# An mLSTM cell followed by mixture-of-depths: TensorE's order written by hand, chunks made ready two steps ahead, gates in one copy

## The chip, the cores and the metric

The kernel runs on one core of a Trainium2 chip. A core has five engines that run side by side, each through its own queue of instructions, and wait for one another by semaphores: TensorE (PE in the profile; its weight loads are listed apart as PEld), VectorE (DVE), ScalarE (ACT), GpSimd (POOL) and SyncE (SP), which here only issues DMAs. The metric is the device time of one execution in microseconds (us); the span of a profile is the part of it from the first to the last instruction of the program.

## What is computed

First an mLSTM cell for 4 batches, 8 heads, 768 positions and a head dimension of 40, then a mixture-of-depths block over rows of 320 (= 8 x 40). Cut to what matters:

```python
for t in range(S):                          # S = 768
    m_new  = maximum(f[t] + m, i[t])
    f_stab = exp(f[t] + m - m_new);  i_stab = exp(i[t] - m_new);  m = m_new
    C = f_stab * C + i_stab * outer(v[t], k[t])        # 40 x 40 per head
    n = f_stab * n + i_stab * k[t]
    y[t] = sigmoid(o[t]) * (C @ q[t]) / maximum(abs(n @ q[t]), 1)
x = y as (4, 768, 320)
scores = x @ w_gate
for b in range(4):
    top = the 128 rows of x[b] with the highest scores
    out[b] = x[b];  out[b, top] += sigmoid(scores[b, top]) * (relu(x[b, top] @ w1) @ w2)   # 320 -> 1024 -> 320
```

## The kernel before

The sequence is cut into chunks of L = 128 positions, so that a batch has NT = 6 chunks and the kernel 24 steps n = (b, c). Within a chunk the recurrence is done as a masked 128 x 128 product per head; between chunks a state C of 41 columns (the 41st carries the normaliser n) is passed on. All the large products are in float32.

**The gates.** `gates(c0, c1)` works for all 32 (batch, head) pairs at once, one pair per partition, by scans on VectorE. Log weights of a pair of positions are the difference of two vectors, a and M. Each is split into three bfloat16 numbers, and the kernel holds the gates four times over (partitions 0 to 127), one copy for each part, so that `operands(u, c)` places them with two matmuls (`pO`, L164), from which ScalarE copies `a_o` (L167) and VectorE makes `M_o` (L168). Three small transpositions (`pc`, L195) turn the remaining factors into columns (`cols`, L197). Gates are set up in three calls: chunk 0, chunks 1 and 2, chunks 3 to 5.

**A step.** `prepare` makes a chunk ready one step ahead: two bfloat16 matmuls `pW` (L220), the exponential `W` on ScalarE (L221), the causal mask on GpSimd (L222), the weighted values `wv` on GpSimd (L227), the transpositions of k and q `pt` (L233) and their copies `T` on ScalarE (L234), and the output gate `so` (L236, L237). `mlstm_chunk` then does:

- `pS` (L250), the product of keys and queries, 64 rows deep; VectorE multiplies it with W into `P` (L252, two instructions);
- `pI` (L261), the part from the state; VectorE scales it into `num` (L264);
- `pC` (L272), the chunk's own part of the next state; GpSimd scales the old state (L275), VectorE adds (L284, in a batch's first chunk a copy, L282);
- `pH` (L289), the part from within the chunk; VectorE adds it to `num` (L293), makes `den` and `rec` (L297 to L300), GpSimd makes `sor` (L302), VectorE makes the row block `x` (L303) and its scores `sc` (L306); GpSimd's queue writes x to the output (L308).

`pI`, `pC` and `pH` share one pool of two PSUM buffers in this order, so that pH takes the buffer of pI once VectorE has read it into `num`. `pt` and `pW` share another pool of two, and all smaller products a third (`ps_m`).

**The second block.** `compare` transposes a chunk's scores (`pb`, L315), ScalarE copies them (L316) and VectorE compares them with the earlier ones (`ge`, L318). Once a batch is complete, during the next batch: `ranks` in step c = 1 (`pcol`, L327; `sel`, L337), `gather` in c = 2 (`pidx`, L347; an indirect DMA brings the 128 rows `xe`, L353), `enter` and the first half of layer 1 in c = 3 (`pX`, L373; `xeT`, L375; `ph`, L386; relu into `hT`, L388), the other half in c = 4, layer 2 in c = 5 (`py`, L394; `ye`, L396; an indirect DMA out, L397). The layer 2 of the third batch is left to the end, where the fourth batch's selection and both its layers follow as a chain.

**What sets the order.** The kernel is written in the Tile framework, which traces the program and then orders the instructions of every engine by priorities and modelled costs. In the kernel before this holds for all engines. TensorE's stream of the kernel before, for instance, mixes transpositions of a later chunk between the `pS` of an earlier one.

Of the kernel before, what the change touches and what calls it, by code (L numbers as in the profile page):

```python
# [27 lines left out]
def kernel(  # L28
# [34 lines left out]
    SLOTS = [(j, min(128, capacity - j)) for j in range(0, capacity, 128)]  # L63
# [3 lines left out]
    AHEAD = 3  # L67

    assert S == NT * L and NT == 6 and D < DP and H == 8 and B == 4 and F_ == NFC * 128 and 0 < capacity < S <= 2048

    const = ctx.enter_context(tc.tile_pool(name="const", bufs=1))
    gate = ctx.enter_context(tc.tile_pool(name="gate", bufs=1))
    ob = ctx.enter_context(tc.tile_pool(name="ob", bufs=2))
# [3 lines left out]
    outp = ctx.enter_context(tc.tile_pool(name="outp", bufs=2))  # L77
    dram = ctx.enter_context(tc.tile_pool(name="dram", bufs=1, space=bass.MemoryType.DRAM))
# [6 lines left out]
    G = [slice(BH * g, BH * (g + 1)) for g in range(4)]  # L85
    f_sb = gate.tile([128, NT, L], FP, name="f_sb")
    i_sb = gate.tile([128, NT, L], FP, name="i_sb")

    def load_f_i(c0, c1):
        for dst, src, eng in ((f_sb, f_gate, nc.sync), (i_sb, i_gate, nc.scalar)):  # L90
            for g in G:
                eng.dma_start(out=dst[g, c0:c1], in_=src.rearrange("b h (c p) -> (b h) c p", p=L)[:, c0:c1])

    ident = const.tile([128, 128], FP, name="ident")
    make_identity(nc, ident)
    load_f_i(0, 1)
# [6 lines left out]
    def load_chunk(b, c):  # L103
        n = (b * NT + c) % NB
        if b * NT + c < NB:
            nc.gpsimd.memset(qk_t[n][:, :, :, D:DP], 0.0)
            nc.gpsimd.memset(v_t[n][:, :, D:DP], 1.0)
        t = slice(c * L, (c + 1) * L)
        for j, src in enumerate((k, q)):
            nc.sync.dma_start(out=qk_t[n][:, j, :, 0:D], in_=src[b, :, t, :].rearrange("h p d -> p h d"))  # L110
        nc.sync.dma_start(out=v_t[n][:, :, 0:D], in_=v[b, :, t, :].rearrange("h p d -> p h d"))
        so = ob.tile([128, H, D], FP, name="so", bufs=NB)
        nc.sync.dma_start(out=so, in_=o_gate[b, :, t, :].rearrange("h p d -> p h d"))
        return qk_t[n], v_t[n], so

    place = [[const.tile([128, 4, 8, 4], BF, name=f"place{x}{u}") for u in range(B // 2)] for x in "Ma"]  # L120
    for j, (own, other, sign) in enumerate(((0, 3, -1.0), (3, 0, 1.0))):
        for u, pl in enumerate(place[j]):
            nc.vector.memset(pl, 0.0)
            nc.vector.memset(pl[0:1, :, other:other + 3, :], 1.0)
            nc.vector.tensor_scalar(out=pl[:, :, own:own + 3, :].rearrange("p g k h -> p k g h"), op0=OP.mult,
                                    in0=ident[:, BH:].rearrange("p (k n g h) -> p k n g h", k=3, g=4, h=4)[:, :, u],
                                    scalar1=sign, scalar2=None)
    which = const.tile([128, 4], FP, name="which")
    nc.vector.tensor_reduce(out=which, in_=ident.rearrange("p (k h) -> p h k", h=4), op=OP.add, axis=AX.X)


    again = const.tile([128, NT, L], BF, name="again")
    low = const.tile([128, NT, L], BF, name="low")
# [4 lines left out]
    F = gate.tile([128, NT, L], FP, name="F")  # L138
    a = gate.tile([128, NT, L], FP, name="a")
    Mg = gate.tile([128, NT, L], FP, name="Mg")  # L140
    m = gate.tile([128, NT + 1], FP, name="m")
    a3 = const.tile([128, NT, L], BF, name="a3")
    M3 = const.tile([128, NT, L], BF, name="M3")

    rest, r, wk = f_sb, F[0:BH], i_sb[0:BH]
    nc.vector.memset(m[:, 0:1], -BIG)
    cols, M_o, a_o = [], {}, {}
# [4 lines left out]
    def split(x3, x, g):  # L152
        nc.vector.tensor_copy(out=x3[:, g], in_=x[:, g])
        nc.vector.tensor_tensor(out=rest[64:128, g], in0=x[64:128, g], in1=x3[64:128, g], op=OP.subtract)
        nc.vector.tensor_copy(out=x3[64:128, g], in_=rest[64:128, g])
        nc.vector.tensor_tensor(out=x3[96:128, g], in0=rest[96:128, g], in1=x3[96:128, g], op=OP.subtract)
        nc.vector.memset(x3[0:BH, g], 1.0)

    def operands(u, c):


        pX = ps_m.tile([128, 2, L], FP, name="pO", tag="m")
        for j, x3 in enumerate((M3, a3)):
            nc.tensor.matmul(pX[:, j, :], place[j][u].rearrange("p g k h -> p (g k h)"), x3[:, c, :], start=True, stop=True)  # L164
        M_o[u, c] = const.tile([128, 4, L], BF, name=f"M_o{u}{c}")
        a_o[u, c] = const.tile([128, L], BF, name=f"a_o{u}{c}")
        nc.scalar.copy(out=a_o[u, c], in_=pX[:, 1, :])  # L167
        nc.vector.tensor_tensor(out=M_o[u, c], in0=pX[:, 0, :].unsqueeze(1).to_broadcast([128, 4, L]), op=OP.mult,  # L168
                                in1=which.unsqueeze(2).to_broadcast([128, 4, L]))

    def gates(c0, c1):
        g, n = slice(c0, c1), c1 - c0
        nc.vector.tensor_tensor_scan(out=flat(F[:, g]), data0=flat(again[:, g]), data1=flat(f_sb[:, g]), initial=0.0,
                                     op0=OP.mult, op1=OP.add)
        nc.vector.tensor_tensor(out=a[:, g], in0=i_sb[:, g], in1=F[:, g], op=OP.subtract)
        nc.vector.tensor_tensor_scan(out=flat(Mg[:, g]), data0=flat(low[:, g]), data1=flat(a[:, g]), initial=0.0,
                                     op0=OP.add, op1=OP.max)
        nc.vector.tensor_tensor_scan(out=m[:, c0 + 1:c1 + 1], data0=Mg[:, g, L - 1], data1=F[:, g, L - 1],
                                     initial=m[:, c0:c0 + 1], op0=OP.max, op1=OP.add)
        mb = m[:, g].unsqueeze(2).to_broadcast([128, n, L])  # L180
        nc.vector.tensor_tensor(out=Mg[:, g], in0=Mg[:, g], in1=mb, op=OP.max)
        nc.vector.tensor_tensor(out=wk[:, g], in0=a[0:BH, g], in1=Mg[0:BH, g, L - 1:L].to_broadcast([BH, n, L]),
                                op=OP.subtract)
        nc.scalar.activation(out=wk[:, g], in_=wk[:, g], func=AF.Exp)
        nc.vector.tensor_tensor(out=r[:, g], in0=mb[0:BH], in1=Mg[0:BH, g], op=OP.subtract)
        nc.scalar.activation(out=r[:, g], in_=r[:, g], func=AF.Exp)
        split(M3, Mg, g)
        split(a3, a, g)
        for c in range(c0, c1):
            operands(0, c)  # L190


            pc = ps_m.tile([128, 3, BH], FP, name="pc", tag="m")
            for j, row in enumerate((wk[:, c, :], r[:, c, :], r[:, c, L - 1:L].to_broadcast([BH, L]))):
                nc.tensor.transpose(pc[:, j, :], row, ident[0:BH, 0:BH])  # L195
            cols.append(const.tile([128, 3, BH], FP, name=f"cols{c}"))
            nc.vector.tensor_copy(out=cols[c], in_=pc)  # L197
# [16 lines left out]
    def prepare(b, c, qk, v1, so):  # L214

        W = work.tile([128, H, L], FP, name="W")
        for h0 in range(0, H, 4):
            rows_in = slice(64 * (b % 2) + 8 * h0, 64 * (b % 2) + 8 * h0 + 32)
            pW = ps_t.tile([128, 4, L], FP, name="pW", tag="t")
            nc.tensor.matmul(pW, a_o[b // 2, c][rows_in], M_o[b // 2, c][rows_in], start=True, stop=True)  # L220
            nc.scalar.activation(out=W[:, h0:h0 + 4, :], in_=pW, func=AF.Exp)  # L221
        nc.gpsimd.affine_select(out=W, in_=W, compare_op=OP.is_ge, fill=0.0, base=0, pattern=[[0, H], [1, L]],  # L222
                                channel_multiplier=-1)
        wv = None
        if c < NT - 1:
            wv = work.tile([128, H, D1], FP, name="wv")
            nc.gpsimd.tensor_tensor(out=wv, in0=v1[:, :, 0:D1], op=OP.mult,  # L227
                                    in1=cols[c][:, 0, b * H:(b + 1) * H].unsqueeze(2).to_broadcast([128, H, D1]))
# [9 lines left out]
        return W, T, wv  # L238

    def mlstm_chunk(b, c, qk, v1, so, W, T, wv, x, sc):  # L240
        hs = slice(b * H, (b + 1) * H)
        k_n = qk[:, 0]


        P = work.tile([128, NP, 2, L], FP, name="P", bufs=2)
        pS = [ps_s.tile([128, NP, L], FP, name="pS") for _ in range(2)]
        for p in range(NP):
            for j in range(2):
                e = HALVES[j]
                nc.tensor.matmul(pS[j][:, p, :], T[e, 0, p, :], T[e, 1, p, :], start=True, stop=True)  # L250
        for j in range(2):
            nc.vector.tensor_tensor(out=P[:, :, j, :], in0=pS[j], op=OP.mult,  # L252
                                    in1=W.rearrange("p (n a) t -> p n a t", a=2)[:, :, j, :])

        C = C_t[(b * NT + c) % 3]
# [31 lines left out]
        for h in range(H):  # L287
            for t in HALVES:
                nc.tensor.matmul(pH[t, h, :], P[:, h // 2, h % 2, t], v1[:, h, :], start=True, stop=True)  # L289
# [11 lines left out]
        sor = work.tile([128, H, D], FP, name="sor")  # L301
# [121 lines left out]

    load(0)
    load_f_i(1, NT)
    gates(0, 1)
    prepared(0)
    load(1)
    gates(1, 3)
# [89 lines left out]
```

## Time and profile before

| | |
|---|---|
| runs | 253.72, 254.0 and 255.19 us, median 254.0 |
| profiled execution | 252.58 us, its span 250.0 us |
| busy in the span | PE 202.1, DVE 166.1, POOL 110.4, ACT 89.9 us |
| mean granted TensorE clock | 0.914 of full speed |
| x of step 0 / 1 / 6 / 12 / 18 / 23 made at | 29.6 / 54.4 / 86.0 / 136.2 / 184.9 / 221.5 us |

Busy shares are means over stages: the first 54 us do two steps, the 168 us that follow do 22, and the last 28 us after x of step 23 are the chain of the last batch. The page divides the span in 40 slices of 6.25 us, one digit each, and for PEclk the digit is the clock that TensorE was granted, in tenths of full speed.

### The profile page before, as it was taken

To read this page: it belongs to the slowest core of one execution; us is meant where nothing else is said; L and a number is where in the kernel's file an instruction comes from. 1 tells how busy PE (TensorE), PEld (TensorE's weight loads), DVE (VectorE), ACT (ScalarE), POOL (GpSimd) and SP (SyncE) were. 2 spreads that over 40 slices of the span, in tenths; PEclk is the share of its full clock that TensorE was granted. 3 is DMA by queue.
4 is the path that set the end of the run, shared out by engine and by line. 5 is a ranking of instruction groups with operands and counts; after the bars stand their busy time and mean duration, and the time that the engine had idled before them with its cause. 6 is when DMAs were issued, how large, how long until landed. Compare 5 with 4: busy or idle time off the path is not lost. (4 is left out here: it accounts for less than half of the span.)

```text
span 250.0 us, 6255 instructions
## 1 busy us (share of the span) xinstructions
PE 202.1 (81%) x2474; PEld 162.7 (65%) x2474; DVE 166.1 (66%) x450; ACT 89.9 (36%) x199; POOL 110.4 (44%) x148
## 2 busy tenths in 40 slices
PE   0175399999788998699999986999999859927890
PEld 0164268778566786589768774987687749915780
DVE  6479986387888798948637888555478795763100
ACT  1243372255345555332544552523534322100010
POOL 4185651256543757532257575332575633221101
PEclk9998555579999999889999999999999999995998
DMA  4999999539864766573346666563250110000000
GB/s 80 180 156 193 216 283 141 65 61 179 156 116 83 136 124 119 120 131 55 81 105 108 126 116 141 111 113 62 79 108 4 42 41 29 26 29 26 26 0 26
DMA packets 102860, 24.94 MB, mean 100 GB/s; under 512 B 100688, under 2 KB 100944, under 8 KB 102832
## 3 DMA queue, kind: packets, MB, share of 16 engines
q1 hardware_dynamic: 100224, 16.13, 42.4%
q0 software_dynamic: 2224, 8.03, 10.0%
q10 hardware_dynamic: 384, 0.39, 0.8%
q8 instruction: 19, 0.31, 0.5%
q14 instruction: 9, 0.07, 0.1%
HBM read 19.96 MB, written 4.59 MB: 98 GB/s over the span
## 5 line engine op out<-in xcount | busy, mean ns | idle before, releaser
L250 PE MATMUL pS<-T 64*128 64x128 f32 x384 | 40.6, 311 | 0.1
L252 DVE TENSOR_TENSOR P<-pS,W 128x512 f32<-128x512 f32 x48 | 31.4, 681 | 12.8 <-PE pS L250 12.7
L250 PEld LDWEIGHTS pS<-T 64*128 64x128 f32 x384 | 31.5, 202 | 9.4 <-issue 7.2
L289 PE MATMUL pH<-v,P 128*64 128x64 f32 x768 | 31.5, 234 | 6.3 <-DVE P L252 3.1
L221 ACT ACTIVATE W<-pW 128x512 f32<-128x512 f32 x48 | 26.9, 596 | 24.8 <-PE pW L220 24.5
L222 POOL TENSOR_SCALAR_AFFINE_SELECT W<-W 128x1024 f32<-128x1024 f32 x24 | 28.2, 1175 | 17.1 <-ACT W L221 16.9
L289 PEld LDWEIGHTS pH<-v,P 128*64 128x64 f32 x768 | 27.0, 145 | 12.4 <-DVE num L264 6.1
L233 PE MATMUL pt<-ident,qk 128*128 128x128 f32 x192 | 32.4, 312 | 3.0 <-ACT W L221 2.7
L302 POOL TENSOR_TENSOR sor<-so,rec 128x320 f32<-128x320 f32 x24 | 17.6, 731 | 32.0 <-DVE rec L300 31.9
L234 ACT COPY T<-pt 128x512 f32<-128x512 f32 x48 | 26.6, 587 | 11.7 <-PE pt L233 11.5
L233 PEld LDWEIGHTS pt<-ident,qk 128*128 128x128 f32 x192 | 24.1, 158 | 7.5 <-ACT W L221 4.8
L227 POOL TENSOR_TENSOR wv<-v,cols 128x328 f32<-128x328 f32 x20 | 15.3, 763 | 31.2 <-PE pC L272 8.5
L386 PE MATMUL ph<-xeT,w 128*128 128x128 f32 x192 | 23.8, 279 | 0.8 <-DVE xeT L375 0.8
L261 PE MATMUL pI<-C,T 128*64 128x128 f32 x320 | 24.3, 290 | 0.0
L386 PEld LDWEIGHTS ph<-xeT,w 128*128 128x128 f32 x192 | 22.3, 192 | 1.6 <-DVE xeT L375 1.0
L316 ACT COPY sb<-pb 128x128 f32<-128x128 f32 x24 | 6.4, 266 | 45.9 <-PE pb L315 45.9
L308 POOL DMA_DIRECT2D out_dram<-x x24 | 14.1, 589 | 18.1 <-DVE x L303 16.5
L303 DVE TENSOR_TENSOR x<-num,sor 128x320 f32<-128x320 f32 x20 | 9.8, 492 | 18.4 <-POOL sor L302 18.4
L275 POOL TENSOR_TENSOR C<-C,cols 128x328 f32<-128x328 f32 x16 | 16.1, 1008 | 12.5 <-DVE C L284 10.4
L394 PE MATMUL py<-w,hT 128*128 128x320 f32 x64 | 20.6, 475 | 0.0
L261 PEld LDWEIGHTS pI<-C,T 128*64 128x64 f32 x320 | 18.6, 142 | 2.9 <-issue 0.6
L318 DVE SCALAR_TENSOR_TENSOR ge<-sb,sc,earlier 128x128 bf16<-128x128 f32 (+5 forms) x24 | 16.9, 704 | 1.9 <-ACT sb L316 1.3
(107 smaller groups left out, 275.7 us busy)
## 6 DMA issues: line engine op xcount, KB each, us to landing
qk<-in_k_dram SPq DMA_DIRECT2D x24, 160.0 KB, 3.5
qk<-in_q_dram SPq DMA_DIRECT2D x24, 160.0 KB, 3.7
v<-in_v_dram SPq DMA_DIRECT2D x24, 160.0 KB, 3.0
so<-in_o_gate_dram SPq DMA_DIRECT2D x24, 160.0 KB, 2.9
out_dram<-x POOLq DMA_DIRECT2D x24, 160.0 KB, 2.6
w<-in_moe_w_dram POOLq DMA_DIRECT2D x1, 1280.0 KB, 7.9
w<-in_moe_w_dram POOLq DMA_DIRECT2D x2, 512.0 KB, 8.1
i_sb<-in_i_gate_dram ACTq DMA_DIRECT2D x4, 80.0 KB, 6.1
```

The lines of the kernel that those rows point to most:

```text
L221: nc.scalar.activation(out=W[:, h0:h0 + 4, :], in_=pW, func=AF.Exp)
L222: nc.gpsimd.affine_select(out=W, in_=W, compare_op=OP.is_ge, fill=0.0, base=0, pattern=[[0, H], [1, L]], channel_multiplier=-1)
L233: nc.tensor.transpose(pt[:, p, :], qk[:, j, 2 * p:2 * p + 2, :].rearrange("s a d -> s (a d)"), ident)
L234: nc.scalar.copy(out=T[:, j], in_=pt)
L250: nc.tensor.matmul(pS[j][:, p, :], T[e, 0, p, :], T[e, 1, p, :], start=True, stop=True)
L252: nc.vector.tensor_tensor(out=P[:, :, j, :], in0=pS[j], op=OP.mult, in1=W.rearrange("p (n a) t -> p n a t", a=2)[:, :, j, :])
L261: nc.tensor.matmul(pI[t, 2 * p:2 * p + 2, :].rearrange("t a d -> t (a d)"), T[:, 1, p, t], C[:, p].rearrange("e a d -> e (a d)"), start=Tr ...
L289: nc.tensor.matmul(pH[t, h, :], P[:, h // 2, h % 2, t], v1[:, h, :], start=True, stop=True)
L302: nc.gpsimd.tensor_tensor(out=sor, in0=so, in1=rec.unsqueeze(2).to_broadcast([128, H, D]), op=OP.mult)
L318: nc.vector.scalar_tensor_tensor(out=ge[:, GE[u]:GE[u + 1]], in0=sb.rearrange("p t l -> p (t l)")[:, 0:n], scalar=sc[:, u:u + 1], in1=earl ...
L386: nc.tensor.matmul(ph[:, f, :], w1[:, j, (f0 + f) * 128:(f0 + f + 1) * 128], xeT[:, j, :], start=(j == 0), stop=(j == NDC - 1))
L394: nc.tensor.matmul(py, hT[:, f, :], w2[:, f, :], start=(f == 0), stop=(f == NFC - 1))
```

## The change

- **TensorE's order by hand**: a manual schedule for TensorE. Its instructions now stand in the order in which the program writes them; the other engines' are still ordered by the framework.
- **Two steps ahead**: `prepare` is parted into `turn` (pt, T, so) and `weigh` (pW, W, wv), `mlstm_chunk` into `scores` (pS, P) and `combine` (the rest). TensorE's order in step n is pS(n), pW(n+2), pI(n), pC(n), pH(n), pb(n-1), pt(n+2), and then a piece of the second block. Loads go four chunks ahead (three before).
- **Gates in one copy**: on 32 partitions, the three parts of a and of M in six tiles; `operands` uses six matmuls in place of two, the constant rows come in by a bias. f and i are loaded once in place of four times. `gates` is called for chunks 0, 1, 2 and 3, 4 and 5. While n + 2 < 6, pO(n+2), pc(n+2) and pW(n+2) all stand at the end of step n, behind pt(n+2). The operands of batches 2 and 3 are made in steps 4 to 9.
- **Layers in five pieces**: layer 1 in pieces of 2, 3 and 3 column blocks of 128 in c = 3, 4, 5, layer 2 in two pieces of four in c = 0 and 1 of the batch after. So layer 2 of batches 0 and 1 falls in batches 2 and 3, and that of batch 2 is parted around `ranks` of the last batch.
- **x by chunk**: a tile for each chunk out of three buffers, in place of one tile for each batch. pH goes through the heads with even ones first.

In VectorE's queue of the changed kernel, as the framework orders it, a step n of 1 to 3 reads P, P, num, C, C, num+pH, ge, den, den, rec, cols(n+2), x, M_o(n+2), score, and then P of step n+1; later steps are the same without cols and M_o, and with the second block's few instructions between.

```diff
-    AHEAD = 3
+    AHEAD = 4
+    ctx.enter_context(tc.manual_schedule(engines={mybir.EngineType.PE}))
-    f_sb = gate.tile([128, NT, L], FP, name="f_sb")
-    i_sb = gate.tile([128, NT, L], FP, name="i_sb")
+    f_sb = gate.tile([BH, NT, L], FP, name="f_sb")
+    i_sb = gate.tile([BH, NT, L], FP, name="i_sb")
...
-            for g in G:
-                eng.dma_start(out=dst[g, c0:c1], in_=src.rearrange("b h (c p) -> (b h) c p", p=L)[:, c0:c1])
+            eng.dma_start(out=dst[:, c0:c1], in_=src.rearrange("b h (c p) -> (b h) c p", p=L)[:, c0:c1])
...
     def gates(c0, c1):
...
-        split(M3, Mg, g)
-        split(a3, a, g)
-        for c in range(c0, c1):
-            operands(0, c)
+        for x, xs in zip((Mg, a), parts):
+            rest = gate.tile([BH, 2, L], FP, name="rest", bufs=2)
+            nc.vector.tensor_copy(out=xs[0][:, g], in_=x[:, g])
+            nc.vector.tensor_tensor(out=rest[:, 0:n], in0=x[:, g], in1=xs[0][:, g], op=OP.subtract)
+            nc.vector.tensor_copy(out=xs[1][:, g], in_=rest[:, 0:n])
+            nc.vector.tensor_tensor(out=xs[2][:, g], in0=rest[:, 0:n], in1=xs[1][:, g], op=OP.subtract)
...
     def operands(u, c):
-        pX = ps_m.tile([128, 2, L], FP, name="pO", tag="m")
-        for j, x3 in enumerate((M3, a3)):
-            nc.tensor.matmul(pX[:, j, :], place[j][u].rearrange("p g k h -> p (g k h)"), x3[:, c, :], start=True, stop=True)
+        pO = ps_m.tile([128, 2, L], FP, name="pO", tag="m")
+        for j in range(2):
+            for part in range(3):
+                nc.tensor.matmul(pO[:, j, :], place[j][u][:, part].rearrange("p g k h -> p (g k h)"),
+                                 parts[j][part][:, c, :], start=(part == 0), stop=(part == 2))
...
+        nc.scalar.activation(out=a_o[u, c], in_=pO[:, 1, :], func=AF.Identity, bias=of[:, 0:1], scale=1.0)
+        nc.vector.scalar_tensor_tensor(out=M_o[u, c], in0=pO[:, 0, :].unsqueeze(1).to_broadcast([128, 4, L]),
+                                       scalar=of[:, 1:2], in1=which.unsqueeze(2).to_broadcast([128, 4, L]),
+                                       op0=OP.add, op1=OP.mult)
...
     for n, (b, c) in enumerate(steps):
-        for ahead in range(1, AHEAD + 1):
+        for ahead in range(2, AHEAD + 1):
             load(n + ahead)
-        if n == 1:
-            gates(3, NT)
         if n == 4:
             load_weights()
-        if NT <= n < 2 * NT and B > 2:
-            operands(1, n - NT)
...
-        prepared(n + 1)
-        mlstm_chunk(b, c, *ready[n], *state[b][0])
+        P = scores(W[n][0], T[n])
+        if NT <= n + 2 < N:
+            W[n + 2] = weigh(*steps[n + 2], *loaded[n + 2])
+        combine(b, c, *loaded[n], T[n], W[n][1], P, state[b][0])
         if n > 0:
             compare(*steps[n - 1], *state[steps[n - 1][0]][1])
+        if n + 2 < N:
+            T[n + 2] = turn(*loaded[n + 2])
+        if n + 2 < NT:
+            if n % 2 == 0:
+                gates(n + 2, n + 4)
+            operands(0, n + 2)
+            columns(n + 2)
+            W[n + 2] = weigh(*steps[n + 2], *loaded[n + 2])
+        if 4 <= n < 4 + NT:
+            operands(1, n - 4)
+        if b > 1 and c < 2:
+            layers[b - 2].second(c * NFC // 2, (c + 1) * NFC // 2)
         if b > 0:
             if c == 1:
-                todo = ranks(b - 1, *state[b - 1][1][2:])
+                sel = ranks(*state[b - 1][1][2:])
             elif c == 2:
-                todo = gather(b - 1, todo)
+                picked = gather(b - 1, sel)
             elif c == 3:
-                todo = enter(todo)
-                layer1(todo, 0)
-            elif c == 4:
-                layer1(todo, 1)
-            elif c == 5 and b < B - 1:
-                layer2(b - 1, todo)
+                layers[b - 1] = Layers(b - 1, *picked)
+                layers[b - 1].first(0, 2)
+            elif c > 3:
+                layers[b - 1].first(3 * c - 10, 3 * c - 7)
     compare(*steps[-1], *state[B - 1][1])
-    picked = gather(B - 1, ranks(B - 1, *state[B - 1][1][2:]))
-    if B > 1:
-        layer2(B - 2, todo)
-    picked = enter(picked)
-    for half in range(2):
-        layer1(picked, half)
-    layer2(B - 1, picked)
+    layers[B - 2].second(0, NFC // 2)
+    sel = ranks(*state[B - 1][1][2:])
+    layers[B - 2].second(NFC // 2, NFC)
+    last = Layers(B - 1, *gather(B - 1, sel))
+    last.first(0, NFC)
+    last.second(0, NFC)
```

## The prediction, as it was put on record

> **What bounds the kernel now.** I read the page's slices first, then the time at which each step's x is made, then the busy time in stretches of one clock window, then the order of time inside one step. The page:
>
> ```profile
> PE   0175399999788998699999986999999859927890
> ...
> DVE  6479986387888798948637888555478795763100
> ...
> PEclk9998555579999999889999999999999999995998
> ```
>
> TensorE is busy nearly everywhere, but from slice 4 to slice 8 (25 to 54 us) at half clock. In that stretch only x of step 1 is made (54.4 us); afterwards a step takes 5.4 to 10 us. So there are three stages with different limits: the start, the steps at full clock, and the last 28.5 us. Why the clock stays at half is seen by cutting the time where it changes (22.56, 53.28, 104.48 us are all whole multiples of 3.413 us apart). Columns: stretch, length, then busy us (instructions) of PE, PEld, DVE, ACT, POOL, then PEclk:
>
> ```profile
> 36.21:39.63 3.42, 3.42 (x25) 2.60 (x24) 1.81 (x3) 1.43 (x3) 0.14 (x1) 0.50 0.97 169
> 43.04:46.45 3.41, 3.41 (x24) 2.77 (x26) 0.82 (x2) 1.09 (x4) 0.00 (x0) 0.50 1.09 144
> 46.45:49.87 3.42, 3.42 (x39) 2.49 (x36) 1.54 (x4) 0.60 (x2) 1.18 (x2) 0.50 0.02 5
> 49.87:53.28 3.41, 3.41 (x18) 2.69 (x17) 2.52 (x7) 1.69 (x5) 1.35 (x2) 0.50 0.29 48
> 53.28:56.69 3.41, 3.31 (x53) 2.68 (x54) 2.85 (x9) 2.02 (x4) 2.53 (x4) 1.00 0.55 94
> 101.07:104.48 3.41, 1.42 (x11) 0.91 (x12) 3.40 (x7) 0.69 (x2) 1.37 (x2) 1.00 0.78 154
> 104.48:107.89 3.41, 3.41 (x40) 3.17 (x40) 3.18 (x12) 2.23 (x6) 2.41 (x2) 0.50 0.13 20
> ```
>
> Four stretches are filled with matmuls to the brim, yet only the fourth is followed by full clock. It is the one with 2.10 us of `pt` and 0.4 us of `pb`, which use all 128 x 128 of the array; the others hold pS, pI and pH, which use 64 rows or 64 columns. I weigh every matmul by the part of the array it uses (pS, pI, pC, pH a half, pW a quarter): the clock rose after stretches of 0.72, 0.93 and 0.76, not after 0.51 to 0.71; it fell after 0.35 and less (101.07 is 0.35), not after 0.39 and more. This rule is mine, from this one trace.
>
> A step at full clock, in order of time:
>
> ```profile
> 199.75 0.49 DVE L303 TENSOR_TENSOR x<-num,sor 128x320 f32<-128x320 f32 x1 [1.59 <-POOL sor L302]
> 200.28 0.49 DVE L306 CUSTOM_DVE_ANT_0 scr<-x,wg 128x320 f32<-128x320 f32 x1
> ...
> 200.70 1.28 DVE L252 TENSOR_TENSOR P<-pS,W 128x512 f32<-128x512 f32 x2
> ...
> 201.90 0.49 DVE L264 TENSOR_TENSOR num<-pI,cols 128x328 f32<-128x328 f32 x1
> ...
> 202.44 1.15 PE L289 MATMUL pH<-v,P 128*64 128x64 f32 x32 [0.93 <-DVE num L264]
> ```
>
> PE had pS ready at 198.3 and then waits 0.93 us for `num`, which stands behind x and the score of the step before on VectorE. So the steps are bound by a ring of both engines, not by PE alone.
>
> [...]`den` at 196.75 took 0.97 us, ending with the 1.09 us mask on GpSimd that began at 196.62; its shortest is 0.17.[...]
>
> **The start.** Loading f and i once takes 12 of 16 DMAs away and lets chunk 0 land earlier (v landed at 11.6). But in the hand order pS(0) comes behind pt, pO, pc, pW of chunk 1 too. VectorE does scans of chunks 1 to 3, twelve placements in place of four, M_o(0), then the splits: with 0.2 to 0.4 us each (rows of L125 to L186) I get M_o(0) at 15.7, W(0) at 17.6, pt(1) to 19.1, M_o(1) to 22.0, pS(0) at 23, and its P at 25.6; x(0) at 32 against 29.6. pS(1) starts at 34, x(1) comes at 45, nine before now.
>
> Then the new stall. In steps 1 to 3 the order is pH(n), pb, pt(n+2), pO(n+2), pc(n+2), pW(n+2), pS(n+1). pW needs M_o(n+2), which on VectorE stands behind cols(n+2), which needs pc, and behind x(n). PE stands still from pc until cols 0.35 + x 0.5 + M_o 0.7 + 0.2 of handing over = 1.75 us later at half clock; at full clock PE is through pc 2.1 us after pH, and waits for x (pH + 3.7) and M_o, 2.3 us. All of pS(n+1) and what follows is queued behind that pW. One step at half clock: pS 1.8, pI 1.85, pC 1.15, pH 1.9, pb 0.3, pt 1.9 (rows of 17.9 to 51.9 us), pO 1.1 (six pairs at 0.19, from the first two at 8.72 and 8.91), pc 0.45, stall 1.75, pW 0.6: 12.8. At full clock: 8.9.
>
> Which clock? By my rule a pt with pH before it raises it where the window ends between 0.8 us before and 1.2 us after pt, 2.0/3.41 = 59% of the steps. But the next window then holds pO on 32 rows, pc and the stall: at most 1.1/3.4 = 0.3, so it falls again. The gain is 0.7 us in 59%: 12.3 a step. pS(4) is at 34 + 3 x 12.3 = 71. Steps 4 and 5 have no such stall: 10.6 and 9.5 at half clock; after a rise 7.2. Between the two, x(6) is at 96.5 against 86.0: **+10.5 us**.
>
> **Steps at full clock.** On PE, start to start: pS 1.09, pW 0.32, pI 0.93, pC 0.54, pH 1.08, pb 0.16, pt 1.02 = 5.14, and the pieces: 2.3 (py, c = 0), 2.9 (py, pcol, c = 1), 0.2, 1.84, 2.08, 2.08. On VectorE: P to num 1.20, num to pH 0.55, pH to num+pH 1.20, that 0.49, `ge` (now behind pH on PE, so never hidden under it) 0.4 to 0.9, den to next P 2.38, in all 6.3 to 6.9[...]. P, num and pH now fit in PE's pW, pI, pC: pS to pH is 1.85 for VectorE and 1.79 for PE. Stalls stay where a piece needs another engine: xeT before ph in c = 3 (0.8), relu before the fifth block in c = 4 (0.85: only two ps_m buffers), sel before P after c = 1 (0.7). Taking the later engine in each step of batch 2: 6.5 + 8.7 + 6.9 + 8.0 + 8.0 + 7.0 = 45.1, now 48.7: **-3.6**. Batch 1 has no py, but M_o (0.68) in four steps on VectorE's ring and 0.7 for pO on PE: 45 at full clock, and 3 for steps at half clock until ph pieces come: 48 against 50.2, **-2.2**. The five steps from x(18) to x(23), now with py but without pt in the last two: 36.0 against 36.6, **-0.6**. Freeing x by chunk moves nothing that PE waits for, I cost it at 0. The earlier loads are free too: a buffer comes free a step before the pt that needs it.
>
> **The end.** Now py of batch 2 (6.67 us, half of it at half clock) runs between pidx and pX:
>
> ```profile
> 226.33 0.32 PE L347 MATMUL pidx<-token,sel 128*128 128x1 f16 x6 [1.25 <-DVE sel L337]
> ...
> 226.51 6.67 PE L394 MATMUL py<-w,hT 128*128 128x320 f32 x16
> ...
> 233.01 0.49 PE L373 MATMUL pX<-ident,xe 128*128 128x128 f32 x3
> ...
> 234.28 5.62 PE L386 MATMUL ph<-xeT,w 128*128 128x128 f32 x48 [0.78 <-DVE xeT L375]
> ```
>
> Parted around ranks, py delays pcol by 0.8 and pidx by 1.7 us, and pX comes 3.9 after pidx (rows reach until 230.13): 0.8 earlier, ye out of the way 0.35. But PE then idles about 3.6 us for the rows, the clock falls, and ph (5.6) begins at half clock[...]: +2.5. Together **+1.4**.
>
> Sum: 10.5 - 2.2 - 3.6 - 0.6 + 1.4 = +5.5. The profiled execution of 252.58 (span 250.0) becomes 258.1; the median of 254.0 lies 1.4 above it, so 259.5 us.
>
> **Bounds of what the trace doesn't show.** Clock of steps 1 to 5: all full gives x(6) at 82 (-4.5), all half with steps 6 to 8 too +18; I take +10.5. Six pO matmuls on 32 rows: as little as the two of now (0.4) or 1.2 at half clock; I take 1.1 and 0.7. Steps at full clock: VectorE's ring 6.4[...] to 7.3 (each den waits like the one above), so -14 to +4 over 17 steps; I take -6.4. The end: -1.2 if the clock holds, +2.5.
>
> **Rivals.** (a) Faster: the clock stays full from step 1 or 2 on, because the array is dense enough between the stalls. Then steps take 8.9, x(6) is at 82, batch 1 takes 45: -4.5 - 5.2 - 3.6 - 0.6 + 1.4 = -12.5, 241.5 us. For it: 53 to 86 us held full clock with windows down to 0.43. Against it: the stall comes in every step, and 101.07 fell with 2.2 us idle. It decides from steps of 10.5 us or less (x(6) by 91). (b) A wash: one step of 1 to 3 and all later ones at full clock, x(6) at 91: 254. (c) Slower still: half clock up to ph in step 9, and no gain in the later steps, den waiting on GpSimd each time: +15 + 1.4 = 270. (d) The hand order does nothing, since VectorE's order binds: then only start and end move, +12, 266.
>
> **How the numbers follow.** Chances: forecast 0.46 (own range 255 to 264), (a) 0.24 with its neighbours up to 251, (b) 0.12, (c) and (d) 0.18. The range 244 to 270 leaves out the faster half of (a) and the tail of (c). About 1% is what a measurement of this kernel can tell from no change. Slower by over 1%: forecast, (c), (d), 0.64; within: (b), 0.12; faster: 0.24.
>
> **What would show it.** Right: PEclk at 5 up to slice 10 or beyond, pW in steps 1 to 3 waiting 1.5 us or more for M_o, x(1) at about 45 and x(6) after 92, steps of batch 2 near 7.5, pX at half clock at the end. Wrong: full clock before 60 us with x(6) by 86, or steps of batch 2 at 8 and more.

## The result, and the profile after

The changed kernel took 262.74 us (median of 261.9 to 264.47), the kernel before 254.17 beside it: a ratio of 1.034, 95% interval 1.028 to 1.040, slower. The execution that was profiled is the slowest of the four, 264.47 us with a span of 262.8, where that of the kernel before was 1.6 us below its median; so the spans differ by 12.8 us and the medians by 8.6. Beside the later experiments the kernel before took 247 to 257 us from one execution to the next, with a granted clock of 0.89 to 0.98, so ratios there are against its undisturbed executions, of 247 to 251 us, and can't be set beside the 1.034.

The page's slices after (TensorE and its clock):

```profile
PE   2257772966995997699999975899797779780991
...
PEclk9999986779798599858999997999999999997598
```

TensorE is no longer full between 25 and 54 us, and yet its clock is no longer at half throughout: up to 60 us it is at half from 31.7 to 35.1, from 41.9 to 48.8 and from 55.6 to 59.0 us, and full between them. At the end (slices 36 and 37, counted from 0) it is at half for longer than before, from 239.9 to 250.1 us against 224.0 to 230.8. Cut at the times at which the instruction that makes x begins (x(6) is the x of step 6):

| stage, us | before | after | predicted change | measured change |
|---|---|---|---|---|
| up to x(6) | 86.0 | 89.2 | +10.5 | +3.2 |
| x(6) to x(12), batch 1 | 50.2 | 51.3 | -2.2 | +1.1 |
| x(12) to x(18), batch 2 | 48.7 | 50.6 | -3.6 | +1.9 |
| x(18) to x(23) | 36.6 | 37.8 | -0.6 | +1.2 |
| x(23) to the end | 28.5 | 34.0 | +1.4 | +5.5 |

The sum has the forecast's sign, but hardly a term has its size. Three rows of the table of waits say where to look (engine, line, what it waited for; total, times, longest):

```profile
ACT so L223 <- DMA so<-in_o_gate_dram: 49.4, 16, 5.7
...
PE pW L233 <- DVE M_o L186: 13.9, 6, 3.2
...
DVE ge L324 <- ACT sb L322: 11.6, 12, 4.4
```

The first was 10.5 us in 7 waits before, the third 1.3 in 2. What they do to a step is seen in order of time, here from x of step 17 to x of step 18:

```profile
182.87 0.37 SPq L111 DMA_DIRECT2D so<-in_o_gate_dram  x1
182.87 0.49 DVE L309 TENSOR_TENSOR x<-num,sor 128x320 f32<-128x320 f32 x1 [0.91 <-POOL sor L307]
...
183.34 0.39 PE L233 MATMUL pW<-M_o,a_o 32*128 32x512 bf16 x2
...
185.77 0.32 PE L321 MATMUL pb<-ident,sc 128*128 128x128 f32 x1
...
186.25 0.47 ACT L223 ACTIVATE so<-so 128x320 f32<-128x320 f32 x1 [3.31 <-DMA so<-in_o_gate_dram]
186.63 1.07 ACT L234 ACTIVATE W<-pW 128x512 f32<-128x512 f32 x2
...
187.26 1.15 PE L220 MATMUL pt<-ident,qk 128*128 128x128 f32 x8 [1.17 <-ACT W L234]
...
187.77 1.09 POOL L235 TENSOR_SCALAR_AFFINE_SELECT W<-W 128x1024 f32<-128x1024 f32 x1 [2.61 <-ACT W L234]
187.94 0.27 ACT L322 COPY sb<-pb 128x128 f32<-128x128 f32 x1
...
188.24 1.43 DVE L324 SCALAR_TENSOR_TENSOR ge<-sb,sc,earlier 128x768 bf16<-128x768 f32 x1 [1.99 <-ACT sb L322]
...
190.99 0.49 DVE L309 TENSOR_TENSOR x<-pH,sor 128x320 f32<-128x320 f32 x1 [0.69 <-POOL sor L307]
```

The load of so at 182.87 begins when the product `sor` of step 17 gives back the buffer. Its chunk is that of step 22. But its tanh, four steps ahead of its use, stands next in ScalarE's queue, as the framework ordered it, and waits for the landing. pW is through at 183.7, and its exponential starts at 186.63; pb is through at 186.1, and its copy starts at 187.94. So TensorE waits 1.17 us for a buffer of pW, VectorE 1.99 us for sb, and GpSimd's mask (L235), late as well, falls on VectorE's `ge`: 1.43 us, where the same instruction took 1.02 on its own (230.62).

### The profile page after: what moved, and what is told of

It is laid out like the page before. It is cut to its first block, busy times and chain, and to the rows that moved or that the text cites. A ratio compares the mean times of both kernels' runs of the same rounds, so it can differ in the third digit from the quotient of the medians.

```text
span 262.8 us, 6342 instructions
## 1 busy us (share of the span) xinstructions
PE 197.5 (75%) x2522; PEld 167.2 (64%) x2522; DVE 164.5 (63%) x461; ACT 91.5 (35%) x205; POOL 108.7 (41%) x148
## 5 line engine op out<-in xcount | busy, mean ns | idle before, releaser
L235 POOL TENSOR_SCALAR_AFFINE_SELECT W<-W 128x1024 f32<-128x1024 f32 x24 | 27.1, 1131 | 39.1 <-ACT W L234 39.0
L220 PE MATMUL pt<-ident,qk 128*128 128x128 f32 x192 | 30.7, 311 | 7.8 <-POOL token_i L439 5.0
L250 PE MATMUL pS<-T 64*128 64x128 f32 x384 | 33.2, 322 | 0.0
L250 PEld LDWEIGHTS pS<-T 64*128 64x128 f32 x384 | 27.9, 219 | 4.0 <-issue 2.8
L380 PE MATMUL ph<-xeT,w 128*128 128x128 f32 x192 | 27.5, 307 | 3.1 <-DVE xeT L372 3.1
L380 PEld LDWEIGHTS ph<-xeT,w 128*128 128x128 f32 x192 | 26.3, 221 | 4.3 <-ACT T L221 2.2
L223 ACT ACTIVATE so<-so 128x320 f32<-128x320 f32 x24 | 11.2, 468 | 50.8 <-DMA so<-in_o_gate_dram 49.4
L324 DVE SCALAR_TENSOR_TENSOR ge<-sb,sc,earlier 128x128 bf16<-128x128 f32 (+5 forms) x24 | 20.3, 844 | 12.1 <-ACT sb L322 11.6
L265 PE MATMUL pI<-C,T 128*64 128x128 f32 x320 | 26.1, 315 | 0.0
L265 PEld LDWEIGHTS pI<-C,T 128*64 128x64 f32 x320 | 20.8, 159 | 4.9 <-issue 4.5
L233 PE MATMUL pW<-M_o,a_o 32*128 32x512 bf16 x48 | 10.6, 437 | 13.9 <-DVE M_o L186 13.9
```

The lines of the kernel that those rows point to most:

```text
L220: nc.tensor.transpose(pt[:, p, :], qk[:, j, 2 * p:2 * p + 2, :].rearrange("s a d -> s (a d)"), ident)
L265: nc.tensor.matmul(pI[t, 2 * p:2 * p + 2, :].rearrange("t a d -> t (a d)"), T[:, 1, p, t], C[:, p].rearrange("e a d -> e (a d)"), start=Tr ...
L324: nc.vector.scalar_tensor_tensor(out=ge[:, GE[u]:GE[u + 1]], in0=sb.rearrange("p t l -> p (t l)")[:, 0:n], scalar=sc[:, u:u + 1], in1=earl ...
L380: nc.tensor.matmul(self.ph[:, f % 4, :], w1[:, j, f * 128:(f + 1) * 128], self.xeT[:, j, :], start=(j == 0), stop=(j == NDC - 1))
```

## The experiments

All begin from the changed kernel unless it is said otherwise. Stages in microseconds of one profiled execution each. How well two executions agree is seen in gather_first, which alters the end alone: up to x(23) it is within 1.3 us of the changed kernel in each stage of this table (2.5 in a single batch), so smaller differences say nothing.

| kernel | time, median | x(6) | x(6) to x(23) | end |
|---|---|---|---|---|
| before | 254.17 | 86.0 | 135.5 | 28.5 |
| after | 262.74 | 89.2 | 139.7 | 34.0 |
| act_hand | 253.3 | 90.5 | 127.2 | 32.8 |
| gather_first | 255.95 | 87.9 | 138.7 | 27.8 |
| pw_behind_ps | 251.25 | 79.4 | 137.3 | 34.2 |
| pb_ahead_of_ph | 265.5 | 85.8 | 143.5 | 33.5 |
| so_in_8 | 256.19 | 88.6 | 130.0 | 32.6 |
| no_hand_order | 253.3 | 83.2 | 135.8 | 33.1 |
| act_hand_pe_planner | 249.55 | 87.5 | 126.5 | 33.4 |
| before_act_hand | 252.51 | 84.8 | 137.3 | 29.3 |
| three_edits | 229.88 | 73.1 | 126.9 | 26.2 |
| three_edits_pe_planner | 236.84 | 82.7 | 125.8 | 29.3 |
| three_edits_vector_hand | 258.92 | 90.4 | 143.6 | 26.5 |

**ScalarE's order by hand (act_hand).**

```diff
-    ctx.enter_context(tc.manual_schedule(engines={mybir.EngineType.PE}))
+    ctx.enter_context(tc.manual_schedule(engines={mybir.EngineType.PE, mybir.EngineType.Activation}))
```

> ScalarE's order is written by hand too, so that the tanh of the output gate (so) of chunk n+2 stands behind the two copies of T(n+2) instead of right after the load of chunk n+4 has been issued. Theory A (the tanh that waits for its load blocks ScalarE's queue: 49.4 us in 16 waits, and behind it stand the copy sb, on which VectorE waits 11.6 us, and W): ScalarE's waits for that load fall below 8 us, VectorE's wait for sb below 3, and the time from x(6) to x(23), 139.7 us, falls by 5 to 9 us; in all 254 to 258. Rival B (TensorE's hand order binds the steps; ScalarE has slack): the waits move to other rows, x(6) to x(23) stays within 2 us of 139.7, in all 261 to 264. The start may move by a microsecond or two either way, since exp of the gates now stands behind T there.

Ratio to before 1.017 (1.009 to 1.025). The steps gave back 12.5 us, more than the 5 to 9 expected; ScalarE's wait for so fell from 49.4 to 0.6 us and VectorE's for sb from 11.6 to 1.7. The start lost 4.9 at x(0) (34.4 us), with exp of the gates behind T. The line moves all of ScalarE's queue; that the tanh is what counted is argued from these waits, and no run moved the tanh alone. Groups between 91 and 200 us show in what the 12.5 consist (busy us, mean ns | idle just before). First the changed kernel, then this one:

```profile
L324 DVE SCALAR_TENSOR_TENSOR ge<-sb,sc,earlier 128x128 bf16<-128x128 f32 (+5 forms) x13 | 12.4, 954 | 5.9 <-ACT sb L322 5.7
...
L302 DVE TENSOR_SCALAR den<-num 128x8 f32<-128x8 f32 x11 | 3.9, 358 | 0.0
```

```profile
L324 DVE SCALAR_TENSOR_TENSOR ge<-sb,sc,earlier 128x128 bf16<-128x128 f32 (+5 forms) x14 | 9.6, 685 | 1.1 <-ACT sb L322 0.6
...
L302 DVE TENSOR_SCALAR den<-num 128x8 f32<-128x8 f32 x12 | 2.0, 165 | 0.0
```

The largest part, 4.8 us, is VectorE idle ahead of `ge` (5.9 against 1.1 us). Further, `ge` is 0.27 us shorter and `den` 0.19 on the average of some 12 steps. In the changed kernel the long ones run beside GpSimd: `ge` beside the late mask (1.29 us at 180.14, where the same instruction took 0.88 in this run), and four `den` of 0.7 us beside wv or the scaling of C, where the other seven took 0.17. That the overlap is what lengthens them is read from these pairs alone.

**More buffers for so (so_in_8).** `ob` with `bufs=8` in place of NB = 5.

> Eight buffers for so in place of five, ScalarE left to the planner: the load of so no longer waits for the product sor of the step before, but comes right after v's load, 2 to 3 us earlier in each step; the planner hoists its tanh as before or further. Theory A (what blocks ScalarE is the time from the release of a buffer to the landing of a load that is used steps later): its wait for so falls from 49.4 to between 10 and 30 us, x(6) to x(23) from 139.7 to between 129 and 136, in all 253 to 260. Rival B (the position of tanh in the queue costs, wherever the load lands): the wait stays over 35 us and x(6) to x(23) over 137.

Ratio 1.037 (1.029 to 1.044). Neither theory: the wait stays at 40.4 us in 19 times (B), and the steps fall to 130.0 (A). The load begins earlier and the framework moves the tanhs further forward, soon to seven steps ahead of their use in place of four; ScalarE is blocked nearly as long, at other places. Between 91 and 200 us VectorE idles 2.9 us ahead of `ge` (5.9 in the changed kernel), and `den` averages 253 ns (358). The size of a wait in the table is not its cost; what stands ready behind it is.

**Without TensorE's hand order (no_hand_order), and ScalarE's alone (act_hand_pe_planner).**

```diff
-    ctx.enter_context(tc.manual_schedule(engines={mybir.EngineType.PE}))
```

> Only the line that gives TensorE's order by hand is left out; the planner orders every engine, with the gates in one copy, the loads four ahead, the layers in five pieces and x by chunk as in the changed kernel. It puts the tanh of so behind sb in part of the steps. Theory A (the hand order of TensorE shortens the steps by itself, and loses only because ScalarE's queue is left to the planner): x(6) to x(23) between 134 and 140, ScalarE's wait for so's load 10 to 40 us, in all 252 to 262. Rival B (the hand order itself costs, the other edits gain): below 250. Rival C (the planner with these edits does worse than by hand): over 264.

```diff
+    ctx.enter_context(tc.manual_schedule(engines={mybir.EngineType.Activation}))
```

> ScalarE's order by hand, TensorE's left to the planner: the counterpart of the run with both by hand (253.3 us, x(6) to x(23) in 127.2). Theory A (both are needed: with so out of ScalarE's way, TensorE's hand order is what makes the steps shorter than before): x(6) to x(23) 132 to 138. Rival B (so alone cost the steps, TensorE's order doesn't matter): 126 to 129.

The first: ratio 1.015 (1.004 to 1.026), steps 135.8, ScalarE's wait for so 37.3 us: inside theory A's ranges. The second: 1.008 (1.003 to 1.013), steps 126.5, as rival B had it, and so against what theory A said of the hand order. With ScalarE's queue free, the steps take 127.2 with TensorE's hand order and 126.5 without; with it blocked, 139.7 and 135.8. So the hand order of TensorE doesn't shorten the steps, and beside the blocked queue they are 3.9 us longer with it.

**ScalarE's order by hand in the kernel before (before_act_hand).**

> The kernel before with one line added: ScalarE's order by hand (its program text: W, T, so of chunk n+1, then sb of n-1), TensorE's by the planner as before. In the changed kernel ScalarE's hand order brought x(6) to x(23) to 127 us whoever ordered TensorE. Theory A (the planner's place for so is what cost the steps, in the kernel before too, which had 10.5 us of waits for so's load and 135.5 us from x(6) to x(23)): 127 to 131 us there. Rival B (the chunks made ready two steps ahead and the layers in five pieces are what makes the short steps possible; one step ahead, W and T come just in time): 134 to 140. The start and the end are as in the kernel before, give or take 3 us, so the whole is 243 to 249 under A and 250 to 256 under B, as far as the clock at the start allows a comparison.

Ratio 1.012 (1.004 to 1.020), steps 137.3: rival B. The kernel before has nothing to gain there. What makes steps of 127 us possible is in the rest of the change (chunks two steps ahead, layers in pieces, x by chunk); these were not parted further.

**The comparison ahead of pH (pb_ahead_of_ph).** `combine` calls `compare` of step n-1 ahead of its pH.

> The comparison of step n-1 (pb, its copy sb, ge) stands ahead of pH(n) in TensorE's order instead of behind it, so that ge can run on VectorE while TensorE does pH. Theory A (ge, 0.4 to 1 us, stands on the ring of VectorE between num+pH and den in every step because pb stands behind pH): steps with c over 0 are 0.4 to 0.7 us shorter, x(6) to x(23) falls by 5 to 8 us, in all 254.5 to 258. Rival B (with ScalarE's queue blocked by so, sb comes no earlier, or ge delays num+pH instead): x(6) to x(23) within 2 us of 139.7, in all 261 to 264. Rival C (pb now waits for the score and holds pH back): 264 to 268.

Ratio 1.067 (1.057 to 1.078); steps 143.5. From the timeline:

```profile
139.97 0.32 PE L323 MATMUL pb<-ident,sc 128*128 128x128 f32 x1
...
141.08 0.47 ACT L223 ACTIVATE so<-so 128x320 f32<-128x320 f32 x1 [5.30 <-DMA so<-in_o_gate_dram]
...
142.91 0.27 ACT L324 COPY sb<-pb 128x128 f32<-128x128 f32 x1
...
143.21 1.12 DVE L326 SCALAR_TENSOR_TENSOR ge<-sb,sc,earlier 128x128 bf16<-128x128 f32 x1 [1.91 <-ACT sb L324]
...
144.37 0.50 DVE L300 TENSOR_TENSOR num<-num,pH 128x328 f32<-128x328 f32 x1
```

pb is through at 140.3, its copy comes at 142.91 behind the tanh, and num+pH, for which pH was ready at 141.94, now stands behind `ge`: 2.4 us lost, as rival B had it. Rival C, whose range the time lies in, is seen as well: pb waits 4.6 us for the score in 3 steps (1.8 in one before the edit). How the 3.8 us of the steps divide between them was not parted, and with ScalarE's queue free this edit was not tried.

**pW behind pS in the first steps (pw_behind_ps).** The call of `weigh` for chunks 2 to 5 moves from the end of step n to behind `scores` of step n+1.

> In the first steps pW of chunk n+2 stands behind pS(n+1) instead of ahead of it. Theory A (TensorE's stalls before pW, 13.9 us for M_o, cost the start): those stalls fall below 5 us, x(6) comes 3 to 7 us earlier than 89.2, in all 255.5 to 260. Rival B (VectorE's chain sets the start: scans, splits, placement and the mask on GpSimd): the stall turns up before pI or pH, x(6) stays within 1.5 us of 89.2, in all 261 to 264.

Ratio 1.005 (0.999 to 1.011). x(6) comes 9.8 us earlier, more than expected, though the waits for M_o only fall from 13.9 to 8.8 us: pS runs in the first part of them. From x(0) to x(4) the steps take 9.0, 9.5, 7.7 and 7.5 us in place of 13.5, 10.3, 10.3 and 10.1, and from 47.3 to 74.6 us the clock is full.

**The gather ahead of the scatter (gather_first).**

```diff
     sel = ranks(*state[B - 1][1][2:])
+    picked = gather(B - 1, sel)
     layers[B - 2].second(NFC // 2, NFC)
-    last = Layers(B - 1, *gather(B - 1, sel))
+    last = Layers(B - 1, *picked)
```

> At the end the row gather of the last batch is issued before the second half of batch 2's second layer, so its scatter stands behind the gather on GpSimd. Theory A (the gather waited for the scatter of batch 2 to land, 2.7 us in GpSimd's queue, and pidx stood behind four more products): pX starts 3.5 to 4.5 us earlier after x(23)[...]: in all 256 to 259.5. Rival B (the loss at the end is the clock alone, the gather is hidden): pX moves by under 1 us, in all 261.5 to 263.5.

Ratio 1.023 (1.012 to 1.034). The end falls from 34.0 to 27.8 us, close to what theory A said. The timeline of the changed kernel, then of this one:

```profile
235.04 0.29 PE L347 MATMUL pidx<-token,sel 128*128 128x1 f16 x6
...
236.08 1.02 POOL L394 DMA_INDIRECT out_dram<-ye,idx  x1 [5.90 <-DVE idx L349]
239.59 1.08 POOL L351 DMA_INDIRECT xe<-out_dram,idx  x1 [2.49 <-issue]
...
242.75 0.88 PE L370 MATMUL pX<-ident,xe 128*128 128x128 f32 x3 [7.41 <-DMA xe<-out_dram,idx]
...
244.28 8.40 PE L380 MATMUL ph<-xeT,w 128*128 128x128 f32 x48 [0.65 <-DVE xeT L372]
```

```profile
231.97 0.30 PE L347 MATMUL pidx<-token,sel 128*128 128x1 f16 x6 [1.25 <-DVE sel L340]
...
232.13 2.40 PE L389 MATMUL py<-w,hT 128*128 128x320 f32 x8
...
232.75 1.06 POOL L351 DMA_INDIRECT xe<-out_dram,idx  x1 [4.80 <-DVE idx L349]
...
235.89 0.52 PE L370 MATMUL pX<-ident,xe 128*128 128x128 f32 x3 [1.36 <-DMA xe<-out_dram,idx]
```

In the changed kernel the scatter of batch 2's rows is issued first, and GpSimd then stands for 2.5 us before the gather of batch 3, which begins 3.5 us after the scatter; the scatters of this trace land 2.5 to 4.3 us after their issue. Both go by `rows(b)`, a view of the output that begins at batch 0, so the one overlaps the other. That the gather waits for the scatter to land is read from this; no run gave the two separate views. TensorE idles 7.41 us in place of 1.36, and begins ph at half clock (0.50 until 250.1 us). The edit also puts pidx ahead of four products of py, which is 0.9 of the 4.7 us by which pX comes sooner after x(23).

**The three edits together (three_edits).** ScalarE by hand, pW behind pS, the gather first; besides, the tanh of so(n+1) is issued at the end of step n, and i of the later chunks is loaded ahead of the first exp.

> The three edits together: ScalarE's order by hand, pW behind pS in the first steps, the gather ahead of the second half of batch 2's second layer; besides, the tanh of so(n+1) is issued at the end of step n (in the start behind W), and i is loaded for the later chunks ahead of the first exp, so that the start doesn't lose the 4 to 5 us that ScalarE's hand order cost at x(0). Theory A (three separate losses, each gone by its own edit): x(6) at 78 to 82, x(6) to x(23) 126 to 129, end 27 to 29, in all 233 to 241 by the profiled execution, 5 to 7% below the kernel before. Rival B (with one loss gone the next ring binds, the gains overlap): x(6) to x(23) 130 or more or x(6) at 85 or more, in all 242 to 249.

Ratio **0.929** (0.923 to 0.934): 229.88 us (227.92 to 233.13, 6 runs), faster than either kernel and than expected: x(6) at 73.1, steps 126.9, end 26.2. Alone, the three edits took 9.8, 12.5 and 6.2 us off the start, the steps and the end; together it is 16.1, 12.8 and 7.8. What the start gains beyond the sum lies in the two further changes or in the edits' combination, which were not parted. The clock:

```profile
PEclk9999999999999999799999999999999999999996
```

It falls in one place and in the last slice (mean 0.984, after: 0.898).

**From there: TensorE's order to the framework (three_edits_pe_planner), and VectorE's by hand too (three_edits_vector_hand).** In the second, the score of step n-1 stands behind num and C of step n, and `ge` behind the reciprocal.

> The kernel with the three edits, but TensorE's order left to the planner. Theory A (TensorE's hand order is needed at the start, where the planner puts other work ahead of pS(1): x(1) was at 49.9 us with it and at 37.5 by hand, and the end, too, where the planner may put the second half of the layer ahead of pidx): x(1) 45 to 50, x(6) 82 to 88, x(6) to x(23) 126 to 129, in all 238 to 248. Rival B (the hand order brings nothing anywhere): x(6) within 3 us of 73, in all 227 to 232.

> From the kernel with the three edits: VectorE's order by hand too, with the score of step n-1 behind num and C of step n instead of ahead of P(n), and ge behind the reciprocal, where VectorE waits for GpSimd's sor anyway. Theory A (VectorE's ring still sets the steps: TensorE waits 11.8 us for num, and score 0.57 and ge 0.4 to 1.0 us stand on the ring): steps with c = 0, 2, 4, 5 become 0.3 to 1 us shorter, TensorE's wait for num falls below 5 us, x(6) to x(23) from 126.9 to between 117 and 123, in all 220 to 226. Rival B (TensorE, busy for 112 of the 127 us, sets the steps): 125 to 128. The start may lose up to 3 us, since the placement of all four operands now stands ahead of the first scan: that would show in x(0) alone.

The first took 236.84 us (231.03 to 239.5, 4 runs): x(1) at 45.8, x(6) at 82.7, steps 125.8, as theory A had them. In the profiled executions the hand order is worth 9.6 us in the start and 3.1 in the end, and nothing in the steps, again. But the one profiled here is the slowest of its four, and the fastest, 231.03 us, lies among those with the hand order; so how much it is worth is not settled. The second took 258.92 us (254.17 to 262.22, 7 runs; ratio 1.021, 1.012 to 1.029), and its slowest execution was profiled. The intended part doesn't work: outside the long steps a chunk takes 7.1 to 8.2 us in batch 2, where it took 6.4 to 9.3. Moved, the score can meet GpSimd's mask (1.53 us at 162.09, where it takes 0.49 elsewhere), and num+pH stands behind it. And some steps are long: 15.7 us from x(0) to x(1), 15.4 from x(2) to x(3), 13.4 from x(15) to x(16), the step behind c = 3:

```profile
166.89 0.48 DVE L371 CUSTOM_DVE_ANT_0 scre<-xe,wg 128x320 f32<-128x320 f32 x1
...
167.92 0.54 DVE L380 COPY xeT<-pX 128x384 f32<-128x384 f32 x1
...
168.60 2.90 PE L388 MATMUL ph<-xeT,w 128*128 128x128 f32 x12 [3.04 <-DVE xeT L380]
```

xeT, ready to be copied at 165.6, stands behind x, the score of the gathered rows and its sigmoid; TensorE waits 3.04 us, pS of the next step (171.43) takes 2.08 us, as much as at half clock in the changed kernel (45.34 to 48.75 us), and P waits 5.08 us for it. In the start the fourteen instructions of `gates` stand in front of a step's own. An order by hand must place the rare instructions too.

## Why the prediction was right, and where its steps were not

The forecast (slower, 259.5 us, range 244 to 270) holds: 262.74. That it comes so near is luck: the start is 7.3 us below its term, the steps 10.6 and the end 4.1 above theirs. Of the signs that the prediction named, the stalls, x(1) and pX at half clock came as said, and x(6) after 92 and a clock at half up to slice 10 did not; of those for being wrong, one came: the steps of batch 2 take 8.4 us, where it said 8 and more. So each term is named.

- **The start.** The stalls came, somewhat longer than worked out: pW waited for M_o 3.15, 2.54 and 2.16 us in steps 1 to 3, against 1.75 to 2.3; x(0) at 29.5 (32 said), x(1) at 43.0 (45). One was not foreseen: pc of step 1 waited 3.41 us for the copy sb to free its buffer (41.33), as sb stood behind a tanh that had waited 5.72 us: ScalarE's queue again. The step that failed is "The gain is 0.7 us in 59%: 12.3 a step", since it rests on my rule that a window must use 0.72 of the array. Steps 1 to 3 took 10.3, 10.3 and 10.1 us: from x(1) to x(4) the clock was at half for 12.6 of 30.7 us, which with the prediction's own 12.8 and 8.9 us makes 10.2 a step, an estimate. Windows of 3.41 us of the changed kernel (stretch, length, then busy us of PE, PEld, DVE, ACT, POOL, then PEclk):

```profile
45.34:48.75 3.41, 3.41 (x32) 3.14 (x32) 1.26 (x2) 1.91 (x4) 1.09 (x1) 0.50 0.17 56
...
110.19:113.60 3.41, 3.41 (x20) 2.76 (x18) 1.58 (x6) 1.80 (x4) 1.00 (x2) 0.50 0.56 98
```

  The first holds 2.08 us of pS and 1.36 of pI, nearly all half-array, 0.5 by my weights, and full clock follows (1.00 from 48.75); so it does after the windows that begin at 31.68, filled with pS, pI and pC, and at 55.58, with pS and pI. Over all thirteen traces, from 15 us on, 77 windows at half clock were busy throughout: the 57 without pO were all followed by full clock, and 5 of the 20 with pO. Of 51 with a gap in TensorE's work 46 were not, one with 0.82 of full-array products among them (231.65 in pw_behind_ps). Five were, after gaps of 0.15 to 0.53 us: 83.40 and 233.58 in so_in_8, 160.89 and 212.08 in pb_ahead_of_ph, 218.71 in three_edits_vector_hand. So my rule was wrong: windows that use half of the array were followed by full clock as well. The second window above is one of the 15 that were busy throughout and not followed by a rise; all of them hold pO, also the four of the kernel before on which my rule was built. pO is in bfloat16, but so is pW, which stands in windows that rose. What about pO keeps the clock down, and which gaps it survives, stays open.
- **The steps at full clock.** Forecast -6.4 over 17 steps, measured +4.2. The arithmetic was good but for a tenth or two (the terms of VectorE's 6.3 to 6.9 us add up to 6.2 to 6.7): with ScalarE's queue in order the three stretches take 46.7, 44.0 and 36.6 us, against 48, 45.1 and 36.0 worked out. The step that failed is "The earlier loads are free too: a buffer comes free a step before the pt that needs it." That is so for pt. It left out the tanh, which the framework puts right behind the load. The prediction followed what stands ahead in a queue on VectorE alone; on ScalarE, W and sb stand behind a load whose chunk is used four steps later: in step 18 the tanh waited 3.31 us for it, and W, whose pW was through at 183.7, began at 186.63, sb, whose pb was through at 186.1, at 187.94. ScalarE's order by hand took 12.5 us off the steps. The reason given for the gain was wrong as well: it isn't TensorE's order (127.2 with, 126.5 without).
- **The end.** Forecast +1.4, measured +5.5. The clock was rightly sized: ph took 8.40 us against 5.62, +2.8 (+2.5 said). The step that failed is "pX comes 3.9 after pidx": it came 7.7 after it (235.04 to 242.75). I counted what is moved on TensorE and VectorE and not on GpSimd's queue, where the scatter now stands first and, as it reads, the gather waits for it.
- **The rivals.** (d), that the hand order does nothing and only start and end move, has the mechanism of the steps right, but with the wrong engine: it is ScalarE's queue that binds, not VectorE's order. (c), with `den` waiting on GpSimd each time, is seen in part: 358 ns on average against 165. (a), a clock that stays up, came true for the start only with pW behind pS: x(6) at 79.4 (82 worked out), and throughout with the three edits, 229.88 us.

## What to carry to other kernels

When one engine's order is written by hand, read the other queues in the new order as well: an instruction that waits for a load belongs behind everything that is ready earlier (here ScalarE's waits for so fell from 49.4 to 0.6 us with its order by hand, and the steps from 139.7 to 127.2). Of two indirect transfers on overlapping views of one tensor, issue the one on the critical chain first: here the gather began 3.5 us after the scatter ahead of it. The total of a wait says little, and what stands ready behind the waiting instruction says what it costs: so_in_8 kept 40.4 of the 49.4 us of waits for so, and its steps took 9.7 us less.

## What the hardware showed that was not expected

- Full clock followed a window that half-array products filled: 45.34 to 48.75 us, 0.5 by weight, clock 1.00 after. It followed one that was not busy throughout as well: 83.40 to 86.81 us in so_in_8, with 0.51 us idle. And the clock stayed at half behind windows without any gap that held 0.82 us of pO (86.30 to 89.71 and 110.19 to 113.60 us in the changed kernel; so, too, with 0.8 us of it, 84.57 in gather_first and 82.38 in pb_ahead_of_ph).
- A mask of 1.09 us on GpSimd, moved by a late exponential on ScalarE, ran beside VectorE's `ge`, which took 1.43 us in place of 1.02: a wait on one engine was paid as a longer instruction on a third.
